# The feed-forward of the first two chunks as one wide pass behind step 4, with weight products spread over steps 0 to 3

## The chip, the core and the metric

The kernel runs on one core of a Trainium2 chip. A core has TensorE (PE in the profile, matrix products; PEld are its weight loads), VectorE (DVE), ScalarE (ACT), GpSimd (POOL) and SyncE (SP, which here issues all the DMAs). Each engine works through its own list of instructions in order, and waits at an instruction until what it needs is there. The metric is the time of one execution on the device, in microseconds; the time given is the median of the runs.

## What is computed

Two layers: attention with a local window and a few global keys, and a feed-forward on its output.

```python
scores = q @ k^T / 8 - slope[h] * dist          # B, H, S, D = 4, 8, 768, 64
keep = (j < n_global) | ((i - j >= 0) & (i - j < n_local))   # 8 and 96
a = softmax(where(keep, scores, -1e9));  x = (a @ v) as [3072, 512]
h = (x @ w1) * (x @ w2)                         # w1, w2: 512 x 1024
out = (h @ w3) @ w_out                          # w3: 1024 x 1024, w_out: 1024 x 512
```

There is no nonlinearity between `w3` and `w_out`, so the kernel forms the product of these two once and multiplies `h` by it. The four weights arrive as float64, 8 bytes a number; q, k and v are float32.

## The kernel before, in words

**Two kinds of work.** The 3072 rows are cut into 12 chunks of 256 rows. A chunk has four pairs of heads, and a *step* is two such pairs of one chunk, so there are 24 steps, two to a chunk. Every third chunk begins a sequence (chunks 0, 3, 6, 9) and has smaller windows. Step s consists of:

- `visit(s)` on PE: the values of step s - 1 (L459, L461; their result `v` is split into `xh` on ACT and `xl` on DVE, L63 and L64), then the scores of step s (L406).
- `rows`: on DVE the bias and the row maxima (L421), on ACT the exponentials (L422).
- `softmax`, called by `scale(s)` in the first steps: DVE forms the reciprocal sums (L427, L428), ACT scales the rows (L434), and the keys and values of step s + 1 are asked for (`loads`).
- `turn(s, 0)` and `turn(s, 1)`: PE transposes the rows of one pair each (L447, L449), ACT copies them to SBUF as `ph` (L451). The PSUM tiles of `turn` (`t`, and `v`, which the values use too) have one buffer each.

The feed-forward of a chunk, or of two chunks together, is a generator, `FeedForward.run`. It yields after each *slice* of work, and `slices(k)` takes k slices, which is how PE's gaps inside a step are filled. With 512 columns (two chunks) a slice is 6 products, with 256 columns it is 12. For each of eight blocks f it forms `m` with w1 (ACT copies it to `a`, L168) and `m` with w2 (DVE multiplies the two, L171, and the result is split into `gh` and `gl`), then it multiplies by the folded weight (L178 to L180). One pass has 48 slices at 512 columns, 24 at 256. Numbers are split into a high and a low part, and each product is three (L161 to L163). The pool of accumulators `m` has two buffers, and the weight products below use the same pool.

**The first steps.** Before any feed-forward the weights have to be made. `convert` loads pieces of 128x512 as float64 and turns them into float32 with three DVE instructions each (L54, L56, L58). `w3(f)` does this for the two pieces of block f of w3, and `w12(f)`, *unit* f, for block f of w1 and of w2; for the latter ACT rounds the high part (`w1h`, `w2h`, L122) and `lows()` has DVE form the low part (L130). `fold(f, ks)` adds the products k of w3 and w_out for block f on PE (L142, eight folds a block); behind the eighth ACT copies the high part (`wh`, L144) and `low(f)` has DVE form the low part (L147). So `low(f)` is the last reader of the accumulator of block f.

**What sets the order.** `first_steps` is a list written by hand. PE follows it throughout; DVE and SP follow it in the first steps; ACT's order there is the scheduler's, and from the step after them on ACT's is by hand too and DVE's and SP's are the scheduler's. SP issues each load at its place in the list, when the buffer that it fills is free: the float64 pieces go into four `stage` slots or two `raws` slots.

Before the change chunks 0 and 1 have a pass of 256 columns each. Chunk 0's begins in step 3, of which `slices` takes ten, and steps 4 to 7 take ten, ten, nine and nine; from step 8 on passes have 512 columns and a step takes twelve (5, 4, 3).

Of the kernel before, what the change touches and what calls it, by code (L numbers as in the profile page):

```python
# [21 lines left out]
NP = H // 2  # L22
NQ = 2
T = NQ * P
# [3 lines left out]
NFC = DF // P  # L28
# [7 lines left out]
STEP = 2  # L36
# [9 lines left out]
def convert(nc, pieces):  # L46


    for dst, raw, src in pieces:
        nc.sync.dma_start(out=dst if src.dtype == F32 else raw, in_=src.bitcast(I32))  # L50
    pieces = [(dst, raw.rearrange("p (n t) -> p n t", t=2)) for dst, raw, src in pieces if src.dtype != F32]

    for dst, w in pieces:
        nc.vector.tensor_scalar(out=dst, in0=w[:, :, 1], scalar1=3, scalar2=0x3FFFFFF8, op0=ALU.logical_shift_left, op1=ALU.bitwise_and)  # L54
    for dst, w in pieces:
        nc.vector.scalar_tensor_tensor(out=dst, in0=w[:, :, 1], scalar=-0x40000000, in1=dst, op0=ALU.bitwise_and, op1=ALU.bitwise_or)  # L56
    for dst, w in pieces:
        nc.vector.scalar_tensor_tensor(out=dst, in0=w[:, :, 0], scalar=29, in1=dst, op0=ALU.logical_shift_right, op1=ALU.bitwise_or)  # L58


def split(nc, hi, lo, x):

    nc.scalar.activation(hi, x, AF.Copy)  # L63
    nc.vector.tensor_tensor(out=lo, in0=x, in1=hi.bitcast(F32), op=ALU.subtract)  # L64


class FeedForward:
# [25 lines left out]
    def next(self, ring, slots):  # L93
        self.turn[ring] += 1
        return slots[(self.turn[ring] - 1) % len(slots)]

    def weights(self, *names):


        pieces, fresh = [], []  # L100
        for kind, *at in names:
            if kind == "w":
                f, n = divmod(at[0], 2)

                raw = self.stage[{3: 0, 5: 2, 6: 0}[f] + n] if f in (3, 5, 6) else self.raws[:, n]
                dst, src = self.t3s[:, at[0] % 4], self.src[n][f]
                fresh.append((n, f, dst.bitcast(F32).rearrange("p (i m) -> p i m", i=NCC)))
            elif kind == "o":
                dst, src = self.wo[:, at[0]], self.w_out[at[0]]
            else:  # L110
                f, z = at
                dst = self.mp.tile([P, PC], I32, tag=self.next(0, "agagoo"), name=f"t3_{f}_{z}")
                src = self.w3t[f, :, z * PC:(z + 1) * PC]
                self.t3[f, z] = dst
            if kind != "w":
                raw = self.next(1, self.stage + self.first)
            pieces.append((dst, raw, src))
        convert(self.nc, pieces)
        self.lows()
        for n, f, x in fresh:  # L120
            hi, lo = (w[:, f] for w in self.w[n])
            self.nc.scalar.activation(hi, x, AF.Copy)  # L122
            self.late.append((lo, x, hi))
        if names[0] == ("o", NFC - 2):

            self.first = []
# [198 lines left out]
def banded(ctx, tc, ff, ns, nt, nf, oki, ident, qk, vx):  # L325
# [139 lines left out]
    n = NC * NP // STEP  # L465
    pairs = lambda s: [divmod(STEP * s + i, NP) for i in range(STEP)]
    work = []
    qrs, vrs, phs, xs = {}, {}, {}, {}

    def slices(k):  # L470
        while k > 0 and work:
            if next(work[0], "end") == "end":
                work.pop(0)
            else:
                k -= 1

    def loads(s, keys=True, vals=True):
        if s < n and keys:
            qrs[s] = [load(*p) for p in pairs(s)]
        if s < n and vals:  # L480
            vrs[s] = [load_values(*p) for p in pairs(s)]

    def visit(s):
        if s:
            c, h0 = pairs(s - 1)[0]
            if h0 == 0 and c % 2 == 0:
                xs[c // 2] = [xp.tile([P, NCC, W], F32R, tag=tag, name=f"{tag}_{c}") for tag in ("xh", "xl")]
            uu = ps_v.tile([P, STEP, T], F32, tag="v", name=f"v_{c}_{h0}")
            for i, p in enumerate(pairs(s - 1)):
                values(uu[:, i], *p, vrs[s - 1][i], phs[s - 1][NQ * i:NQ * (i + 1)])  # L490
        ps = [scores(*p, t) for p, t in zip(pairs(s), qrs[s])] if s < n else []
        if s:
            x2 = xs[c // 2]
            xc = [x[:, :, c % 2 * T:][:, :, :T] for x in x2]
            split(nc, *(x[:, h0:h0 + STEP] for x in xc), uu)
            if h0 + STEP == NP and c < 2:
                work.append(ff.run(c, *xc, c * T, T))
            elif h0 + STEP == NP and c % 2:
                work.append(ff.run(c, *x2, (c - 1) * T, W))
        return ps  # L500

    def all_rows(s, ps):
        return [rows(*p, x) for p, x in zip(pairs(s), ps)]

    def turn(s, i, prs):

        phs.setdefault(s, []).extend(flip(*pairs(s)[i], j, prs[i][0]) for j in range(NQ))

    def first_steps():


        ff.more_stages(xp)
        nc.sync.dma_start(out=nt, in_=ns.bitcast(I32).partition_broadcast(P))
        for x in sc[0] + sc[1]:
            nc.vector.memset(x, 0.0)
        biases()
        ff.weights(("t", 0, 0))
        ff.weights(("o", 0))
        ff.fold(0, 0)
        ff.weights(("t", 1, 0), ("t", 2, 0))  # L520
        ff.fold(1, 0)
        ff.fold(2, 0, pool=(ps_v, "v"))
        ff.weights(("o", 1), ("o", 2))
        for k in (1, 2):
            for f in range(3):
                ff.fold(f, k)
        ff.weights(("o", 3), ("t", 0, 1))
        for f in range(3):
            ff.fold(f, 3)
        ff.weights(("t", 1, 1), ("t", 2, 1))  # L530
        loads(0, vals=False)
        ff.weights(("o", 4), ("o", 5))
        ps = visit(0)
        for k in (4, 5):
            for f in range(3):
                ff.fold(f, k)
        ff.weights(("o", 6), ("o", 7))
        loads(0, keys=False)
        prs = all_rows(0, ps)
        for f in range(3):  # L540
            ff.fold(f, 6, 7)

        def w3(f):
            ff.weights(("t", f, 0), ("t", f, 1))

        def w12(f):
            ff.weights(("w", 2 * f), ("w", 2 * f + 1))

        def scale(s):
            for p, r in zip(pairs(s), prs):  # L550
                softmax(*p, *r, nc.scalar)
            loads(s + 1)

        def fold_and_turn(f, s):
            ff.fold(f, 0, 1, 2, 3)
            turn(s, 0, prs)
            ff.fold(f, 4, 5, 6)
            turn(s, 1, prs)
            ff.fold(f, 7)

        w3(3)
        scale(0)
        ff.low(0)
        w3(4)
        ff.low(1)
        ff.low(2)
        w3(5)
        w12(0)
        fold_and_turn(3, 0)
        ff.lows()  # L570
        w3(6)
        prs = all_rows(1, visit(1))
        ff.low(3)
        ff.fold(4, *range(NFC))
        w12(1)
        scale(1)
        ff.lows()
        w3(7)
        ff.low(4)
        fold_and_turn(5, 1)  # L580
        w12(2)
        ff.lows()
        ff.low(5)
        prs = all_rows(2, visit(2))
        ff.fold(6, *range(NFC))
        w12(3)
        scale(2)
        ff.lows()
        ff.low(6)
        fold_and_turn(7, 2)  # L590
        w12(4)
        ff.lows()
        w12(5)
        ff.lows()
        ff.low(7)
        prs = all_rows(3, visit(3))
        w12(6)
        slices(2)
        scale(3)
        ff.lows()  # L600
        w12(7)
        slices(SLICES[3][0] - 2)
        ff.lows()
        for i in range(STEP):
            turn(3, i, prs)
            slices(SLICES[3][i + 1])
        fits(nc, ff.mp, nf, oki)


    SLICES = [()] * 3 + [(4, 4, 2)] * 3 + [(4, 3, 2)] * 2 + [(5, 4, 3)] * (n - 8)  # L610
    with tc.manual_schedule(engines={mybir.EngineType.PE}):
        with tc.manual_schedule(engines={mybir.EngineType.DVE, mybir.EngineType.SP}):
            first_steps()
        with tc.manual_schedule(engines={mybir.EngineType.Activation}):
            for s in range(4, n + 1):
                rs = all_rows(s, visit(s))
                if s == n:
                    break

                slices(2)  # L620
                for p, r in zip(pairs(s), rs):
                    softmax(*p, *r, nc.vector)
                loads(s + 1)
                slices(SLICES[s][0] - 2)
                for i in range(STEP):
                    turn(s, i, rs)
                    slices(SLICES[s][i + 1])
            slices(10 ** 6)


# [43 lines left out]
```

## Time and profile before

| what | value |
|---|---|
| median of three runs | 596.42 us (596.34 to 596.58) |
| the profiled execution: its time | 596.74 us |
| its span, first to last instruction | 595.0 us |
| PE busy | 573.7 us |
| DVE busy | 260.9 us |
| ACT busy | 284.4 us |
| moved by DMA | 54.01 MB |
| PE's idle time by its waits | 14.7 us, 11.2 of them at the start |

A row of a timeline is: start in us from the span's beginning, length in us, engine, line, operation, output and inputs, shape, count of merged instructions, and in brackets how long the engine idled before and what released it. The start of the next row tells how long an instruction really held its engine, since the lengths of neighbours overlap. A product of full float32 is two records. A row of the busy times by stretch has, behind the stretch, its length and the busy us of PE, PEld, DVE, ACT and POOL (with counts), the granted clock of PE as a share of full speed, the share of the DMA engines and GB/s. A row of the waits says who waited at which line for whom: us in total, times, the longest. Lines are those of the kernel before; up to L490 the changed kernel has the same numbers.

### The profile page before, as it was taken

The numbers are of one execution on the slowest core, as the hardware profiler recorded it, in microseconds if no ns is written. First come the engines' busy times: TensorE is split into PE (matmuls) and PEld (weight loads), VectorE is DVE, ScalarE is ACT, GpSimd is POOL, SyncE is SP. The second block draws the span as 40 slices with busy tenths as digits, with TensorE's granted clock in tenths as the row PEclk, the third lists the DMA queues.
The fourth block names the chain that finished last, engine by engine and source line by source line (L and its number), as shares of the span: only waits on it lengthen the run. The fifth ranks groups of instructions, "written<-read, shape, count | busy, mean of one in ns | idle before, by whom it ended". The sixth has DMA issues, their size and how long they took to land. (4 is left out here: it accounts for less than half of the span.)

```text
span 595.0 us, 9954 instructions
## 1 busy us (share of the span) xinstructions
PE 573.7 (96%) x3872; PEld 459.2 (77%) x3872; DVE 260.9 (44%) x851; ACT 284.4 (48%) x777; POOL 1.3 (0%) x10
## 2 busy tenths in 40 slices
PE   2999998999999999999999999999999999999995
PEld 0444568989988888888888888888888888888884
DVE  8999998531434424404533322541343353112200
ACT  3056677644656446526635544653553663422210
POOL 0000000000000000000000000000000000000000
PEclk9999998999999999999999999999999999999999
DMA  8897752221133202212210330120331020000011
GB/s 305 302 356 238 275 194 106 81 82 33 49 97 98 79 2 78 81 49 69 79 59 21 115 113 3 63 63 14 120 97 49 30 80 19 36 18 1 0 37 40
DMA packets 23240, 54.01 MB, mean 91 GB/s; under 512 B 2704, under 2 KB 4752, under 8 KB 23184
## 3 DMA queue, kind: packets, MB, share of 16 engines
q1 hardware_dynamic: 23184, 53.29, 26.2%
q8 instruction: 32, 0.52, 0.4%
q14 instruction: 24, 0.20, 0.1%
HBM read 46.99 MB, written 6.29 MB: 90 GB/s over the span
## 5 line engine op out<-in xcount | busy, mean ns | idle before, releaser
L422 ACT ACTIVATE pr<-pr,mx 128x232 f32<-128x232 f32 (+1 forms) x192 | 88.4, 462 | 48.7 <-DVE mx L421 48.7
L171 DVE TENSOR_TENSOR g<-m,a 128x512 f32<-128x512 f32 x48 | 33.2, 691 | 133.2 <-PE m L163 132.5
L161 PE MATMUL m<-xh,w1h 128*128 128x512 f32 (+1 forms) x224 | 84.6, 378 | 0.0
L163 PE MATMUL m<-xh,w1l 128*128 128x512 f32 (+1 forms) x224 | 81.0, 361 | 0.0
L162 PE MATMUL m<-xl,w1h 128*128 128x512 f32 (+1 forms) x224 | 80.9, 361 | 0.0
L161 PE MATMUL m<-xh,w2h 128*128 128x512 f32 (+1 forms) x224 | 80.8, 361 | 0.0
L162 PE MATMUL m<-xl,w2h 128*128 128x512 f32 (+1 forms) x224 | 80.4, 359 | 0.0
L163 PE MATMUL m<-xh,w2l 128*128 128x512 f32 (+1 forms) x224 | 80.4, 359 | 0.0
L178 PE MATMUL o<-wh,gh 128*128 128x512 f32 x192 | 76.6, 399 | 0.0
L63 ACT ACTIVATE gh<-g 128x512 fp32r<-128x512 f32 x48 | 30.3, 630 | 94.2 <-DVE g L171 93.6
L180 PE MATMUL o<-wh,gl 128*128 128x512 f32 x192 | 74.9, 390 | 0.0
L179 PE MATMUL o<-wl,gh 128*128 128x512 f32 x192 | 74.9, 390 | 0.0
L142 PE MATMUL w<-wo,t 128*128 128x512 f32 x128 | 59.6, 615 | 11.7 <-DVE wo L58 11.2
L64 DVE TENSOR_TENSOR xl<-v,xh 128x512 fp32r<-128x512 f32 x24 | 16.6, 690 | 120.4 <-ACT xh L63 120.3
L451 ACT ACTIVATE ph<-t 128x512 f32<-128x512 f32 (+1 forms) x96 | 50.1, 558 | 30.1 <-PE t L449 18.9
L142 PEld LDWEIGHTS w<-wo,t 128*128 128x128 f32 x128 | 24.0, 196 | 40.4 <-issue 24.2
L421 DVE CUSTOM_DVE_ANT_0 pr<-s,biasw 128x232 f32<-128x232 f32 x160 | 53.4, 394 | 0.0
L161 PEld LDWEIGHTS m<-xh,w1h 128*128 128x128 f32 x224 | 42.7, 191 | 8.5 <-issue 3.3
L64 DVE TENSOR_TENSOR gl<-g,gh 128x512 fp32r<-128x512 f32 x48 | 33.2, 692 | 33.2 <-ACT gh L63 33.2
L161 PEld LDWEIGHTS m<-xh,w2h 128*128 128x128 f32 x224 | 42.3, 189 | 7.0 <-issue 0.7
L163 PEld LDWEIGHTS m<-xh,w1l 128*128 128x128 f32 x224 | 42.6, 190 | 6.5
L162 PEld LDWEIGHTS m<-xl,w2h 128*128 128x128 f32 x224 | 42.3, 189 | 6.4
(84 smaller groups left out, 815.7 us busy)
## 6 DMA issues: line engine op xcount, KB each, us to landing
qr<-qk SPq DMA_DIRECT2D x32, 312.0 KB, 4.1
vr<-vx SPq DMA_DIRECT2D x32, 256.0 KB, 2.9
stage<-w3t SPq DMA_DIRECT2D x15, 512.0 KB, 6.4
out_dram<-ot SPq DMA_DIRECT2D x24, 256.0 KB, 2.0
raws<-w SPq DMA_DIRECT2D x10, 512.0 KB, 5.6
qr<-qk SPq DMA_DIRECT2D x16, 260.0 KB, 3.3
vr<-vx SPq DMA_DIRECT2D x16, 192.0 KB, 2.6
stage<-w SPq DMA_DIRECT2D x6, 512.0 KB, 6.2
```

The costliest lines, as they stand in the source:

```text
L64: nc.vector.tensor_tensor(out=lo, in0=x, in1=hi.bitcast(F32), op=ALU.subtract)
L142: nc.tensor.matmul(ps, lhsT=self.t3[f, z][:, i * P:(i + 1) * P].bitcast(F32), rhs=self.wo[:, k].bitcast(F32), start=k == 0, stop=k == NFC - 1)
L161: nc.tensor.matmul(ps[:, z], lhsT=mh, rhs=xh[:, i], start=i == 0, stop=False)
L162: nc.tensor.matmul(ps[:, z], lhsT=mh, rhs=xl[:, i], start=False, stop=False)
L163: nc.tensor.matmul(ps[:, z], lhsT=ml, rhs=xh[:, i], start=False, stop=i == NCC - 1)
L171: nc.vector.tensor_tensor(out=g, in0=ps, in1=a, op=ALU.mult)
L178: nc.tensor.matmul(ps, lhsT=gh[:, f, ts], rhs=self.wh[:, f], start=f == 0, stop=False)
L179: nc.tensor.matmul(ps, lhsT=gh[:, f, ts], rhs=self.wl[:, f], start=False, stop=False)
L180: nc.tensor.matmul(ps, lhsT=gl[:, f, ts], rhs=self.wh[:, f], start=False, stop=f == NFC - 1)
L421: nc.vector.tensor_tensor_reduce(out=pr[:, j, u, w0:], in0=ps[u][:, j, w0:UW], in1=bias, scale=-SCALE, scalar=3.0e38, op0=ALU.add, op1=ALU ...
L422: nc.scalar.activation(pr[:, j, u, w0:], pr[:, j, u, w0:], AF.Exp, bias=m, scale=-1.0, accum_out=sm[:, j, u:u + 1])
L451: nc.scalar.activation(ph[:, :, :nk], pt[:, :, :nk], AF.Copy)
```

## The change

Chunks 0 and 1 no longer have passes of their own: one pass of 512 columns serves both, like all the others, and it begins after `visit(4)`. Every step from 4 on takes 5, 4 and 3 slices, and step 3 takes none. `fold_and_turn` gives way to `around`, which puts given folds ahead of, between and behind the two turns of a step; the folds of blocks 3 to 7 are spread over steps 0 to 3. In the list, units of w1 and w2 and blocks of w3 stand at other places, and units 2, 4 and 5 use the `stage` slots where 3, 5 and 6 did.

```diff
-                raw = self.stage[{3: 0, 5: 2, 6: 0}[f] + n] if f in (3, 5, 6) else self.raws[:, n]
+                raw = self.stage[{2: 0, 4: 2, 5: 0}[f] + n] if f in (2, 4, 5) else self.raws[:, n]
...
-            if h0 + STEP == NP and c < 2:
-                work.append(ff.run(c, *xc, c * T, T))
-            elif h0 + STEP == NP and c % 2:
+            if h0 + STEP == NP and c % 2:
                 work.append(ff.run(c, *x2, (c - 1) * T, W))
...
+        def around(s, a, b, e):
+            for i, part in enumerate((a, b, e)):
+                for f, k0, k1 in part:
+                    ff.fold(f, *range(k0, k1 + 1))
+                if i < STEP:
+                    turn(s, i, prs)
         w3(3)
         scale(0)
         ff.low(0)
+        ff.low(2)
         w3(4)
         ff.low(1)
-        ff.low(2)
+        around(0, [(3, 0, 1)], [(3, 2, 2)], [(3, 3, 4)])
         w3(5)
+        prs = all_rows(1, visit(1))
+        ff.fold(3, 5, 6, 7)
+        ff.low(3)
+        scale(1)
         w12(0)
-        fold_and_turn(3, 0)
+        around(1, [(4, 0, 4)], [(4, 5, 5)], [(4, 6, 7)])
         ff.lows()
         w3(6)
-        prs = all_rows(1, visit(1))
-        ff.low(3)
-        ff.fold(4, *range(NFC))
+        prs = all_rows(2, visit(2))
+        ff.low(4)
+        scale(2)
         w12(1)
-        scale(1)
+        around(2, [(5, 0, 7), (6, 0, 0)], [(6, 1, 1)], [(6, 2, 3)])
         ff.lows()
         w3(7)
-        ff.low(4)
-        fold_and_turn(5, 1)
         w12(2)
+        prs = all_rows(3, visit(3))
         ff.lows()
         ff.low(5)
-        prs = all_rows(2, visit(2))
-        ff.fold(6, *range(NFC))
+        scale(3)
         w12(3)
-        scale(2)
+        around(3, [(6, 4, 7), (7, 0, 3)], [(7, 4, 5)], [(7, 6, 7)])
         ff.lows()
         ff.low(6)
-        fold_and_turn(7, 2)
         w12(4)
         ff.lows()
+        ff.low(7)
+        prs = all_rows(4, visit(4))
...
-    SLICES = [()] * 3 + [(4, 4, 2)] * 3 + [(4, 3, 2)] * 2 + [(5, 4, 3)] * (n - 8)
+    SLICES = (5, 4, 3)
...
-            for s in range(4, n + 1):
+            for s in range(5, n + 1):
```

Behind `visit(4)` the new list has units 5, 6 and 7 among step 4's slices and turns.

Three places show what that does to the engines' lists. The first is DVE around `low(5)`, the difference of block 5 (its accumulator is `w_518` in the kernel before). Before, from `low(4)` to the split behind visit 2:

```order
L147 TENSOR_TENSOR wl<-w_465,wh 128x512
L54 TENSOR_SCALAR t3s<-raws 128x512 x2
L56 SCALAR_TENSOR_TENSOR t3s<-raws,t3s 128x512 x2
L58 SCALAR_TENSOR_TENSOR t3s<-raws,t3s 128x512 x2
L130 TENSOR_TENSOR w1l<-t3s,w1h 128x512
L130 TENSOR_TENSOR w2l<-t3s,w2h 128x512
L147 TENSOR_TENSOR wl<-w_518,wh 128x512
L64 TENSOR_TENSOR xl_410<-v_2_565,xh_409 128x2x256
```

And in the change, where the accumulator of block 5 is `w_603`:

```order
L421 ISA pr_3_714,mx_3_715<-s_107,biasw 128x232
L421 ISA mx_3_715 128x1
L130 TENSOR_TENSOR w1l<-t3s,w1h 128x512
L130 TENSOR_TENSOR w2l<-t3s,w2h 128x512
L147 TENSOR_TENSOR wl<-w_603,wh 128x512
L427 TENSOR_SCALAR sm_2_705<-sm_2_705 128x4
```

It stood ahead of the rows of step 2 and now stands behind those of step 3 (the first two lines are the last of these rows).

The second place is PE behind a visit's last scores. Before, behind visit 2, with block 6 as `w_618` and block 7 as `w_661`:

```order
L406 MATMUL s_107<-qr_1_499 64x168
L142 MATMUL w_618<-wo,t_6_0_399 128x512 x4
L142 MATMUL w_618<-wo,t_6_1_400 128x512 x4
L142 MATMUL w_661<-wo,t_7_0_507 128x512 x4
L447 MATMUL t_0_0_666<-ident,pr_0_596 128x128
```

In the change, behind visit 3, with block 6 as `w_613` and block 7 as `w_763`:

```order
L406 MATMUL s_107<-qr_3_587 64x168
L142 MATMUL w_613<-wo,t_6_1_510 128x512 x4
L142 MATMUL w_763<-wo,t_7_0_648 128x512 x4
L447 MATMUL t_2_0_768<-ident,pr_2_703 128x128
L449 MATMUL t_2_0_768<-ident,pr_2_703 128x128
```

Block 7's folds moved from step 2 to step 3. In both programs the first fold of block 7 waits for `low(5)` on DVE, whose accumulator it takes over.

The third place is PE in the first pass of the feed-forward, where `m` with w1 is followed by `m` with w2 (the first number in a name, the chunk or the pass, is left out). Before, block 0 of chunk 0:

```order
L161 MATMUL m_0_0_793<-xh_409,w1h 128x256
L162 MATMUL m_0_0_793<-xl_410,w1h 128x256
L163 MATMUL m_0_0_793<-xh_409,w1l 128x256
L161 MATMUL m_0_1_852<-xh_409,w2h 128x256
L162 MATMUL m_0_1_852<-xl_410,w2h 128x256
```

In the change, block 1 of the pass for both chunks:

```order
L161 MATMUL m_1_0_950<-xh_383,w1h 128x512
L162 MATMUL m_1_0_950<-xl_384,w1h 128x512
L163 MATMUL m_1_0_950<-xh_383,w1l 128x512
L161 MATMUL m_1_1_981<-xh_383,w2h 128x512
L162 MATMUL m_1_1_981<-xl_384,w2h 128x512
```

The products are twice as wide and half as many. In the program of the change the first product of `m_1_1` waits for ACT's copy of `m_1_0`, whose accumulator it takes over.

More of the change, by code (lines that the diff above doesn't have):

```diff
@@ L552, in scale @@
             loads(s + 1)
[L554 to L559, printed above, removed]
+        def around(s, a, b, e):
[4 more added lines that the diff above has]
+                    turn(s, i, prs)
         w3(3)
@@ L563, in first_steps @@
         ff.low(0)
+        ff.low(2)
         w3(4)
         ff.low(1)
-        ff.low(2)
+        around(0, [(3, 0, 1)], [(3, 2, 2)], [(3, 3, 4)])
         w3(5)
+        prs = all_rows(1, visit(1))
+        ff.fold(3, 5, 6, 7)
+        ff.low(3)
+        scale(1)
         w12(0)
-        fold_and_turn(3, 0)
+        around(1, [(4, 0, 4)], [(4, 5, 5)], [(4, 6, 7)])
         ff.lows()
         w3(6)
-        prs = all_rows(1, visit(1))
-        ff.low(3)
-        ff.fold(4, *range(NFC))
+        prs = all_rows(2, visit(2))
+        ff.low(4)
+        scale(2)
         w12(1)
-        scale(1)
+        around(2, [(5, 0, 7), (6, 0, 0)], [(6, 1, 1)], [(6, 2, 3)])
         ff.lows()
         w3(7)
-        ff.low(4)
-        fold_and_turn(5, 1)
         w12(2)
+        prs = all_rows(3, visit(3))
         ff.lows()
         ff.low(5)
-        prs = all_rows(2, visit(2))
-        ff.fold(6, *range(NFC))
+        scale(3)
         w12(3)
-        scale(2)
+        around(3, [(6, 4, 7), (7, 0, 3)], [(7, 4, 5)], [(7, 6, 7)])
         ff.lows()
         ff.low(6)
-        fold_and_turn(7, 2)
         w12(4)
         ff.lows()
+        ff.low(7)
+        prs = all_rows(4, visit(4))
         w12(5)
+        slices(2)
+        scale(4)
         ff.lows()
-        ff.low(7)
-        prs = all_rows(3, visit(3))
         w12(6)
-        slices(2)
-        scale(3)
+        slices(SLICES[0] - 2)
         ff.lows()
+        turn(4, 0, prs)
+        slices(SLICES[1])
         w12(7)
-        slices(SLICES[3][0] - 2)
+        turn(4, 1, prs)
+        slices(SLICES[2])
         ff.lows()
-        for i in range(STEP):
-            turn(3, i, prs)
-            slices(SLICES[3][i + 1])
         fits(nc, ff.mp, nf, oki)
-    SLICES = [()] * 3 + [(4, 4, 2)] * 3 + [(4, 3, 2)] * 2 + [(5, 4, 3)] * (n - 8)
+    SLICES = (5, 4, 3)
     with tc.manual_schedule(engines={mybir.EngineType.PE}):
@@ L623, in banded @@
                 loads(s + 1)
-                slices(SLICES[s][0] - 2)
+                slices(SLICES[0] - 2)
                 for i in range(STEP):
                     turn(s, i, rs)
-                    slices(SLICES[s][i + 1])
+                    slices(SLICES[i + 1])
             slices(10 ** 6)
```

## The prediction

> **What bounds the kernel now.** First the page: who is busy, and when in the span.
>
> ```profile
> span 595.0 us, 9954 instructions
> PE 573.7 (96%) x3872; PEld 459.2 (77%) x3872; DVE 260.9 (44%) x851; ACT 284.4 (48%) x777; POOL 1.3 (0%) x10
> PE   2999998999999999999999999999999999999995
> DVE  8999998531434424404533322541343353112200
> ```
>
> TensorE is full from the second slice to the last but one, so what counts is PE time that is not work. But DVE at 44% is a mean over two regimes. The table of busy time by stretch shows them, and where PE's clock fell:
>
> ```profile
> 75.00:90.00 15.00, 15.00 (x125) 10.63 (x124) 14.71 (x39) 11.54 (x28) 0.00 (x0) 1.00 0.52 188
> 105.00:120.00 15.00, 15.00 (x161) 14.39 (x160) 7.40 (x37) 8.64 (x27) 0.00 (x0) 1.00 0.25 80
> ...
> 96.00:98.00 2.00, 2.00 (x11) 2.00 (x10) 2.00 (x4) 2.00 (x6) 0.00 (x0) 0.51 0.00 0
> ```
>
> Up to 90 us both engines are full (DVE 14.71 of 15); after 105 us DVE has half its time free. PE's waits, all of them but two:
>
> ```profile
> PE w L142 <- DVE wo L58: 11.2, 1, 11.2
> PE t L447 <- ACT pr L434: 2.4, 2, 2.1
> ```
>
> The 11.2 us stand at the start, which the change leaves alone. The 2.1 us stand at step 3's first transpose. So in the first 90 us DVE's conversions and attention rows are a second chain, just hidden behind PE's folds and the feed-forward of chunk 0. This is the cover that the change takes apart.
>
> **The change, from the end backwards.** The scores of each visit mark the steps on PE:
>
> ```profile
> 108.64 1.37 PE L406 MATMUL s<-qr 64*64 64x168 f32 x32
> 181.05 1.37 PE L406 MATMUL s<-qr 64*64 64x168 f32 x32
> 352.09 1.37 PE L406 MATMUL s<-qr 64*64 64x168 f32 x32
> 436.53 1.37 PE L406 MATMUL s<-qr 64*64 64x168 f32 x32
> 86.93 0.28 PE L161 MATMUL m<-xh,w1h 128*128 128x256 f32 x1
> ...
> 89.32 0.28 PE L163 MATMUL m<-xh,w1l 128*128 128x256 f32 x1
> ```
>
> They are those of steps 4, 8, 16 and 20. Steps 4 to 7 take 181.05 - 108.64 = 72.41 us now, with 38 slices of feed-forward. In the change they hold 48, with the same chunks and the same turns as steps 16 to 19 have now: 436.53 - 352.09 = 84.44 us. That adds 12.03 us, and step 3 loses its ten slices, 120 products of 256 columns at (89.32 - 86.93) / 20 = 0.120, 14.3 us. The wide form so saves about 2.3 us. From step 8 on nothing changes. Without new waits the change breaks even when step 4's scores start at 108.64 - 12.03 = **96.6 us**; every microsecond by which they are later is lost. The old 2.1 us wait lies before 108.64 and is in this figure.
>
> [...]
>
> **When do step 4's scores start?** Unit costs on DVE, ACT and PE:
>
> ```profile
> 55.01 0.77 DVE L54 TENSOR_SCALAR t3s<-raws 128x512 int32<-128x512 int32 x2
> 58.08 0.18 DVE L427 TENSOR_SCALAR sm<-sm 128x4 f32<-128x4 f32 x1
> 58.66 0.66 DVE L130 TENSOR_TENSOR w1l<-t3s,w1h 128x512 fp32r<-128x512 f32 x1
> 69.58 0.39 DVE L421 CUSTOM_DVE_ANT_0 pr<-s,biasw 128x232 f32<-128x232 f32 x1
> 72.13 0.76 DVE L54 TENSOR_SCALAR t3s<-stage 128x512 int32<-128x512 int32 x2
> ```
>
> ```profile
> 36.74 0.58 ACT L144 ACTIVATE wh<-w 128x512 fp32r<-128x512 f32 x1
> 73.39 0.47 ACT L422 ACTIVATE pr<-pr,mx 128x232 f32<-128x232 f32 x1
> 76.26 3.13 ACT L434 ACTIVATE pr<-pr,sm 128x232 f32<-128x232 f32 x8
> 79.29 1.06 ACT L451 ACTIVATE ph<-t 128x512 f32<-128x512 f32 x2
> 80.25 0.63 ACT L122 ACTIVATE w1h<-t3s 128x512 fp32r<-128x512 f32 x1
> ```
>
> ```profile
> 48.34 10.57 PE L142 MATMUL w<-wo,t 128*128 128x512 f32 x24
> 77.93 0.27 PE L447 MATMUL t<-ident,pr 128*128 128x128 f32 x1
> 78.80 2.74 PE L142 MATMUL w<-wo,t 128*128 128x512 f32 x6
> 83.21 0.45 PE L459 MATMUL v<-ph,vr 128*64 128x128 f32 x4
> 85.17 1.37 PE L406 MATMUL s<-qr 64*64 64x168 f32 x32
> 86.47 0.39 PE L161 MATMUL m<-xh,w1h 128*128 128x256 f32 x1
> ```
>
> DVE: a converted pair of pieces 3.07 (55.01 to 58.08), a step's sums 0.56, a difference (L147, L130, L64) 0.60, a step's rows 2.55, or 2.1 in a first chunk. ACT: the exponentials end 4.2 after the rows begin (73.39 + 0.47 against 69.58), the scalings of a step take 3.0, a copy of L451 or L144 0.5, of L122 0.55. PE: a fold is two records of 0.44, 0.88; a turn 0.87; values 1.96; scores 1.30.
>
> DVE first. Both kernels are alike to 35.3 us. From there to the end of low(5) the new order has seven converted pairs (products 4 to 7, units 0 to 2 of w1 and w2) 21.5, three steps of rows 7.2, fifteen differences (six low, three lows of two, xl at three visits) 9.0 and the sums of steps 1 and 2 1.1: 38.8 us of work. It also waits where it did not, because work that stood between is gone:
> - low(2) now follows low(0), but ACT's copy of w_2 starts at 36.74 and ends at 37.3: 1.4.
> - low(3) follows step 1's rows at once, and its copy stands behind eight exponentials on ACT: 2.3.
> - lows of unit 0: the raw pieces' DMAs are now behind step 2's keys and values on SP's queue, which wait for visit 1 (issued near 47 and not at 35, landing near 52.5 by the 5.6 us of their row below), and the copies of L122 stand behind four copies of turns, which wait for PE: 2.5.
> - sums of step 2, for its exponentials: 0.9.
> - lows of unit 1, in the same place: 2.3.
>
> ```profile
> raws<-w SPq DMA_DIRECT2D x10, 512.0 KB, 5.6
> 35.33 0.66 DVE L147 TENSOR_TENSOR wl<-w,wh 128x512 fp32r<-128x512 f32 x1
> ```
>
> These are 9.4 us. So low(5), counted from low(0) in the second row, ends near 35.3 + 38.8 + 9.4 = 83.5, with some handovers of 0.1 **84.0 us**. No row shows these waits; if ACT and the DMAs were always ready they are 0 and low(5) ends near 74, PE waits for nothing; with each half longer it ends near 88.7. I take the walk's sum, as each is set by an order of instructions that is fixed.
>
> Now PE. Its own work brings it through visit 3 (values from 72.9, after the last copy of step 2's turn) and the rest of product 6 to about 79.7. Product 7 uses the accumulator of product 5, which low(5) reads: PE stands until 84.1, **4.4 us**. Queued behind this wait are turn 3, visit 4 and all of the feed-forward. Then four folds 3.5, a turn 0.87, two folds 1.75, a turn 0.87, two folds 1.75, values 1.96 and 0.1: 94.9 us.
>
> Then the clock. How did it answer an idle PE so far?
>
> ```profile
> 94.62 0.47 PE L447 MATMUL t<-ident,pr 128*128 128x128 f32 x1 [2.14 <-ACT pr L434]
> 97.67 0.41 PE L161 MATMUL m<-xh,w1h 128*128 128x256 f32 x1
> 98.05 0.28 PE L163 MATMUL m<-xh,w1l 128*128 128x256 f32 x1
> 11.23 2.07 PE L142 MATMUL w<-wo,t 128*128 128x512 f32 x2 [11.23 <-DVE wo L58]
> 13.71 11.07 PE L142 MATMUL w<-wo,t 128*128 128x512 f32 x22 [0.41 <-DVE t L58]
> ```
>
> After 2.14 us idle PE ran at half clock from 94.6 to 97.95 (0.51 in the stretch from 96 to 98): 1.65 us lost. After the 11.23 us at the start 24 records took 13.1 us and not 10.6: 2.5 lost. A wait of 4.4 us will cost at least the first; I take 1.65, and 0 and 2.5 as ends. Scores of step 4: 94.9 + 1.65 = **96.6 us**, just the break-even.
>
> [...]
>
> **Step 4 itself** has two new waits. Turn 4 comes after five slices (6.9 us after the feed-forward's start near 97.9), and the scalings of step 4 on ACT stand behind the exponentials, a first copy L168 and two L122 copies that wait for unit 5's conversion: last scaling near 106.1, so about 0.55 us. Then m_1_1 waits for the copy a of m_1_0, since it got the accumulator that m_1_0 just held (g of m_0, which would free the other, is behind unit 6's conversion on DVE); that copy stands behind two scalings' rest and two L451 copies: 1.4 us. Together 1.95; ends 0 (if the scalings come early) and 3.5. Units 5 to 7 are wanted from about 130 us on and are ready by 121: nothing, hidden behind the products of units 0 to 4.
>
> **Sum.** 595.0 + (96.6 - 96.6) + 1.95 = 597.0 us of span. The profiled execution took 596.74 outside its span of 595.0, but the runs' median is 596.42: add 1.42. **598.4 us**, 0.33% slower.
>
> **Rivals.**
> - *The waits shrink* (faster): if ACT and the DMAs answer in 6 us for the 9.4, low(5) ends at 80.6, PE idles 1 us, and its clock holds: 94.9 - 3.4 = 91.5, span 595 - 5.1 + 1.95 = 591.9, 593.3 us. For it: DVE was full to 90 us, so its order was served well. Against: each wait above has an instruction ahead of it on ACT. It decides from a saving of 3 us on.
> - *The clock holds or step 4 does not wait* (same): without the 1.65, or without the 1.95, 596.4 to 596.8. For it: one wait alone shows the fall, and where it stood may have mattered. Against: 2.14 us were enough.
> - *DMAs late too* (much slower): the pieces of units 1, 3 and 6 stand behind 1.1 MB of keys and values; 1.5 us more at unit 1 and the long loss of the clock, 0.85: 600.8 us.
> [...]
>
> **Chances.** Forecast 0.50, waits shrink 0.13, same 0.27, late DMAs 0.10. About 0.2% (1.2 us) is what can be told from no change: faster is the first rival, 0.13; the same the second, 0.27; slower the rest, 0.60. The 80% range goes from 595.3 (1.5 us of the waits less, and no loss of the clock) to 600.7.
>
> **What would show it.** Right: in PE's waits a fold (L142) that waits about 4 us for DVE's L147 near 80 us; a granted clock near 0.5 for some 3 us behind it; step 4's scores at 96 to 97 us and step 8's some 86.4 later; in DVE's waits L147 for ACT's L144 and L130 for L122, together some 8 us. Wrong: low(5) before 81 us, no wait of PE above 2 us, or step 4's scores before 95.

## The result and the profile after

The changed kernel takes 600.42 us (median of 4 runs, 598.36 to 600.81), the kernel before, run beside it on the same chip, 596.5 us (596.34 to 596.7): a ratio of 1.0061, 95% interval 1.0047 to 1.0076. It is slower. The forecast was 598.4 us; the profiled execution took 598.36, the other three 2 us more, and the experiments have to say why.

The page of the changed kernel, to be read beside the page of before:

```profile
span 596.5 us, 9571 instructions
PE 572.5 (96%) x3680; PEld 447.3 (75%) x3680; DVE 260.6 (44%) x847; ACT 287.2 (48%) x781; POOL 1.3 (0%) x10
PE   2999979999999999999999999999999999999995
DVE  8997898764224425304434323542343452112200
```

PE is busy 1.2 us less (572.5 against 573.7) in a span 1.5 us longer: a hole has come into the sixth slice. The waits of PE from 35 us on:

```profile
PE w L142 <- DVE wl L147: 4.3, 1, 4.3
PE m L161 <- ACT a L168: 1.4, 2, 1.1
PE t L447 <- ACT ph L451: 0.6, 2, 0.3
```

The old wait at step 3's transposes (2.1 us, L447 for L434) is gone. In its place block 7's first fold waits for low(5). The timeline of PE has that fold and the scores of steps 3, 4, 5 and 8:

```profile
74.20 1.37 PE L406 MATMUL s<-qr 64*64 64x168 f32 x32
83.48 5.40 PE L142 MATMUL w<-wo,t 128*128 128x512 f32 x8 [4.28 <-DVE wl L147]
95.96 1.37 PE L406 MATMUL s<-qr 64*64 64x168 f32 x32
108.21 0.50 PE L161 MATMUL m<-xh,w2h 128*128 128x512 f32 x1 [1.11 <-ACT a L168]
119.50 1.37 PE L406 MATMUL s<-qr 64*64 64x168 f32 x32
182.87 1.37 PE L406 MATMUL s<-qr 64*64 64x168 f32 x32
```

Step 4's scores start at 95.96, 0.65 us ahead of the break-even of 96.61. Steps 4 to 7 take 182.87 - 95.96 = 86.91 us, where 84.44 was the figure without waits: 2.47 more. From step 8 on the span is 0.32 shorter (413.63 against 413.95). Sum: -0.65 + 2.47 - 0.32 = +1.5 us, the whole difference of the spans. (Since the three parts make up the span, they add up whatever the break-even is. The 0.32 lies behind step 20: steps 8 to 19 take 255.47 us here and 255.48 before.)

The granted clock stands in the busy times by stretch (behind the stretch its length, then PE, PEld, DVE, ACT, POOL, the clock, the DMA share, GB/s):

```profile
82.00:84.00 2.00, 0.52 (x1) 0.30 (x2) 1.93 (x8) 2.00 (x8) 0.00 (x0) 0.99 1.00 389
84.00:86.00 2.00, 2.00 (x4) 0.92 (x3) 1.55 (x4) 2.00 (x6) 0.00 (x0) 0.50 1.02 416
86.00:88.00 2.00, 2.00 (x4) 0.76 (x4) 1.90 (x4) 1.94 (x5) 0.00 (x0) 0.65 1.01 414
```

PE works at half clock right behind the wait, for some 3.4 us. And DVE's waits between 35 and 90 us, the chain that makes low(5) late (all but 0.45 of the 3.8 us stand ahead of low(5)):

```profile
DVE t3s L54 <- DMA raws<-w: 3.8, 5, 1.1
DVE wl L147 <- ACT wh L144: 3.6, 2, 2.2
DVE sm L427 <- ACT pr L422: 0.9, 1, 0.9
DVE w2l L130 <- ACT w2h L122: 0.3, 1, 0.3
```

### The profile page after: what moved, and what is told of

Same layout as the page of the kernel before. It is cut to its first block, busy times and chain, and to the rows that moved or that the text cites. A ratio compares the mean times of both kernels' runs of the same rounds, so it can differ in the third digit from the quotient of the medians.

```text
span 596.5 us, 9571 instructions
## 1 busy us (share of the span) xinstructions
PE 572.5 (96%) x3680; PEld 447.3 (75%) x3680; DVE 260.6 (44%) x847; ACT 287.2 (48%) x781; POOL 1.3 (0%) x10
## 4 chain that ended last, share of the span: by engine, by line
PE 82%; DVE 11%; ACT 4%; DMA 2%; issue 1%; DVEq 0%; ACTq 0%
PE m L161 14%; PE m L162 14%; PE m L163 14%; PE o L178 7%; PE o L180 7%; PE o L179 7%; PE s L406 4%; PE v L459 4%; PE t L447 3%; PE t L449 3%; PE v L461 3%; DVE t L56 2%; DVE t L58 2%; PE w L142 1%; DVE pr L421 1%; ACT pr L422 1%
## 5 line engine op out<-in xcount | busy, mean ns | idle before, releaser
L161 PE MATMUL m<-xh,w1h 128*128 128x512 f32 x192 | 78.9, 411 | 0.3 <-ACT a L168 0.3
L142 PE MATMUL w<-wo,t 128*128 128x512 f32 x128 | 62.1, 630 | 15.9 <-DVE wo L58 11.1
L161 PE MATMUL m<-xh,w2h 128*128 128x512 f32 x192 | 74.8, 390 | 1.1 <-ACT a L168 1.1
L163 PE MATMUL m<-xh,w1l 128*128 128x512 f32 x192 | 75.2, 392 | 0.0
L162 PE MATMUL m<-xl,w1h 128*128 128x512 f32 x192 | 75.1, 391 | 0.0
L162 PE MATMUL m<-xl,w2h 128*128 128x512 f32 x192 | 74.8, 390 | 0.0
L163 PE MATMUL m<-xh,w2l 128*128 128x512 f32 x192 | 74.7, 389 | 0.0
L64 DVE TENSOR_TENSOR xl<-v,xh 128x512 fp32r<-128x512 f32 x24 | 16.6, 692 | 113.8 <-ACT xh L63 113.8
L142 PEld LDWEIGHTS w<-wo,t 128*128 128x128 f32 x128 | 24.3, 200 | 44.8 <-issue 23.3
L421 DVE CUSTOM_DVE_ANT_0 pr<-s,biasw 128x232 f32<-128x232 f32 x160 | 53.6, 396 | 0.0
L184 ACT ACTIVATE ot<-o 128x512 f32<-128x512 f32 x24 | 14.3, 595 | 71.7 <-PE o L180 61.2
L64 DVE TENSOR_TENSOR gl<-g,gh 128x512 fp32r<-128x512 f32 x48 | 33.2, 693 | 33.7 <-ACT gh L63 33.7
L434 ACT ACTIVATE pr<-pr,sm 128x232 f32<-128x232 f32 (+1 forms) x116 | 44.7, 462 | 1.1 <-DVE sm L427 1.1
L161 PEld LDWEIGHTS m<-xh,w1h 128*128 128x128 f32 x192 | 36.1, 188 | 10.6 <-issue 3.7
L161 PEld LDWEIGHTS m<-xh,w2h 128*128 128x128 f32 x192 | 36.0, 188 | 9.1 <-ACT a L168 1.5
```

The source lines that it names most:

```text
L142: nc.tensor.matmul(ps, lhsT=self.t3[f, z][:, i * P:(i + 1) * P].bitcast(F32), rhs=self.wo[:, k].bitcast(F32), start=k == 0, stop=k == NFC - 1)
L161: nc.tensor.matmul(ps[:, z], lhsT=mh, rhs=xh[:, i], start=i == 0, stop=False)
L162: nc.tensor.matmul(ps[:, z], lhsT=mh, rhs=xl[:, i], start=False, stop=False)
L163: nc.tensor.matmul(ps[:, z], lhsT=ml, rhs=xh[:, i], start=False, stop=i == NCC - 1)
L421: nc.vector.tensor_tensor_reduce(out=pr[:, j, u, w0:], in0=ps[u][:, j, w0:UW], in1=bias, scale=-SCALE, scalar=3.0e38, op0=ALU.add, op1=ALU ...
L434: nc.scalar.activation(x, x, AF.Copy, scale=r)
```

## The experiments

In e4, e8_best, e8b, e9 and e12, which issue some transfers apart from their conversion, the lines of the views are higher by up to 10 (L152 for L142), in e2 by 1.

All were timed against the kernel before, in alternation on the same chip. Ratios are to it.

| run | median us | before | ratio, 95% | PE's main waits from 35 us on in the profile, us |
|---|---|---|---|---|
| the change | 600.42 | 596.50 | 1.0061 (1.0047 to 1.0076) | low(5) 4.3, copy a 1.4 |
| e1_again | 599.93 | 596.14 | 1.0067 (1.0055 to 1.0079) | low(5) 4.4, copy a 1.4 |
| e2_refold | 597.74 | 596.14 | 1.0032 (1.0021 to 1.0044) | low(5) 0.8, copy a 1.4 |
| e3_low5 | 600.63 | 596.14 | 1.0070 (1.0052 to 1.0088) | turn 3 2.4, g 2.0 |
| e4_unit2 | 598.30 | 596.14 | 1.0034 (1.0022 to 1.0047) | copy ph 2.1, xl 2.0, g 1.4 |
| e6_pool | 597.69 | 596.58 | 1.0017 (1.0004 to 1.0030) | low(5) 3.6, copy a 1.1 |
| e8b_order | 600.80 | 596.58 | 1.0073 (1.0050 to 1.0096) | copies a 3.6, turn 3 2.1, xl 1.2 |
| e8_best | 598.50 | 596.58 | 1.0045 (1.0032 to 1.0058) | copies a 2.6, turns 1.7, xl 1.5 |
| e9_raws | 599.82 | 596.58 | 1.0070 (1.0043 to 1.0096) | low(5) 2.7, turns 1.6, g 1.4 |
| e10_later | 594.58 | 596.38 | 0.9960 (0.9944 to 0.9976) | copies a 1.3 |
| e11_short | 595.69 | 596.38 | 0.9984 (0.9972 to 0.9995) | low(5) 1.0, g 1.7 |
| e12_short | 594.92 | 596.38 | 0.9978 (0.9964 to 0.9991) | copies a 2.4, turns 1.6 |

**e1_again: the same kernel, for its scatter.** No edit.

> The changed kernel once more, unaltered, to see what sets its two levels (its profiled execution took 598.36 us, the three others 600.4 to 600.8, with mean clocks of 0.994 against 0.991). Theory (clock): the DVE walk and the wait of PE at block 7's first fold (4.3 us) are the same in every execution, and only the stretch at half clock behind it differs: about 3.4 us in the short level, about 7.5 us in the long one. Most times at 600.4, some at 598.4; a profile of the long level shows step 4's scores near 98.0 and the wait still at 4.3. Rival (transfers): in the long level the pieces of unit 1 land later and low(5) ends some 2 us later; a profile of the long level shows a wait of PE above 6 us and the cold stretch unchanged.

Six runs took 598.88 to 600.56; so there are no two clean levels but a scatter of 2 us, and all six lie above the one that was profiled first. The profile of this one (599.12 us):

```profile
83.67 5.94 PE L142 MATMUL w<-wo,t 128*128 128x512 f32 x8 [4.42 <-DVE wl L147]
...
96.69 1.37 PE L406 MATMUL s<-qr 64*64 64x168 f32 x32
```

```profile
80.00:82.00 2.00, 0.00 (x0) 0.00 (x0) 2.00 (x13) 2.00 (x10) 0.00 (x0) 0.85 1.01 361
82.00:84.00 2.00, 0.33 (x1) 0.33 (x2) 1.93 (x7) 2.00 (x10) 0.00 (x0) 0.50 1.02 399
84.00:86.00 2.00, 2.00 (x3) 0.85 (x3) 1.67 (x5) 2.00 (x7) 0.00 (x0) 0.50 1.02 416
86.00:88.00 2.00, 2.00 (x3) 0.68 (x2) 1.90 (x4) 2.00 (x6) 0.00 (x0) 0.50 1.00 406
88.00:90.00 2.00, 2.00 (x10) 1.14 (x9) 2.00 (x5) 0.31 (x1) 0.00 (x0) 0.94 0.14 55
```

The wait is the same 4.4 us, but the clock falls while PE still waits, near 81.4, and stays down to 88.2: 6.8 us and not 3.4. What the loss costs PE is read from the end of the wait to step 4's scores, the same work in four kernels and five profiles: 10.78 us in e2_refold, where the clock holds, 12.48 in the change's profile, 13.02 here (96.69 - 83.67), 13.66 in e6_pool and 13.81 in e9_raws. So the price is **1.7 to 3.0 us**, and it differs between the two profiles of the same kernel too (1.70 and 2.24). That is for the clock theory, but with a smaller difference (0.5 us) than it had named, and no execution above 600 us was traced. Nor is the clock all of the scatter: the run of 598.88 has a mean clock of 0.996 and is longer than that of 598.36 with 0.994.

**e2_refold: more work in the wait.** The first four products of block 6 are done once more (the first time closed as a sum of its own, `stop` at product 3).

```diff
-        around(3, [(6, 4, 7), (7, 0, 3)], [(7, 4, 5)], [(7, 6, 7)])
+        around(3, [(6, 0, 7), (7, 0, 3)], [(7, 4, 5)], [(7, 6, 7)])
```

> The first four products of block 6 are done twice, the second time where PE now stands and waits for low(5): 3.5 us more work on PE, nothing else changed. Theory (clock): the idle time falls from 4.3 to about 0.8 us, low(5) still ends near 83.4, the clock holds, so the 1.7 us of the short level and the 3.8 us of the long one are both saved: span 594.8, time 596.6, and all runs on one level. Rival 1 (the clock does not hang on this wait): span 596.5 and times of 598.4 to 600.8 as in the change. Rival 2 (the waits come from PE's own order): the added work is paid in full, 602 us and more.

597.74 us, 2.2 less than the change in the same session, with 3.5 us more work on PE. All six mean clocks are 0.997 to 0.999, against 0.991 to 0.996 of the change. In the profile (L143 is L142 here):

```profile
83.46 3.70 PE L143 MATMUL w<-wo,t 128*128 128x512 f32 x8 [0.77 <-DVE wl L148]
94.24 1.37 PE L407 MATMUL s<-qr 64*64 64x168 f32 x32
```

The fold starts at 83.46 as before, since low(5) sets it, and step 4 is 1.7 us earlier, all of it clock. That the wait itself is DVE's and the loss behind it is the clock's is thereby shown; the time is 1.1 us above the 596.6 expected.

**e3_low5: the late instruction moved up.**

```diff
         ff.lows()
+        ff.low(5)
         w3(7)
         w12(2)
         prs = all_rows(3, visit(3))
         ff.lows()
-        ff.low(5)
         scale(3)
```

> low(5) is moved ahead of product 7's conversion, so it ends near 72.8 and not 83.4. Theory (the stall moves on): PE's wait of 4.3 us for low(5) is gone, but turn 3 then waits for its scalings, which stand behind rows of step 3 that have become 0.6 us later: a wait of 2.2 to 3.2 us at L447 for L434 near 82.7, and the clock falls behind it as it did after 2.1 us in the kernel before. Step 4's scores near 94.5, span 595.0, time 596.9 at the short level and 599 at the long one. Rival (low(5) is the whole cause): no new wait, clock holds, scores of step 4 near 90.0, span 590.5, time 592.4.

600.63 us, no gain. PE's timeline:

```profile
85.85 0.34 PE L447 MATMUL t<-ident,pr 128*128 128x128 f32 x1 [2.37 <-ACT pr L434]
95.16 1.37 PE L406 MATMUL s<-qr 64*64 64x168 f32 x32
108.61 0.50 PE L161 MATMUL m<-xh,w2h 128*128 128x512 f32 x1 [1.99 <-DVE g L171]
```

The stall went where it was expected, to turn 3, with 2.37 us, and took the clock along (0.51 from 86 to 88 us). A second one was not expected: with low(5) elsewhere the pool gives m_1_1 the accumulator that g of m_0 frees, and g stands behind unit 6's conversion; 1.99 us idle there were enough for a second stretch at half clock (0.50 from 110 to 112).

**e4_unit2: one conversion later.** `w12(2)` goes behind `scale(3)`; its transfers are issued at the old place.

> Unit 2 of w1 and w2 is converted behind step 3's rows, low(5) and sums, and not ahead of them; its transfers are issued where they were. Theory (DVE's total is the bound, not the place of one instruction): low(5) ends near 79.2 and PE waits for nothing in step 3, so step 4's scores start near 90.0; but DVE's work up to low(7) is the same sum, so step 4's xl and rows come near 95 and 98: the feed-forward's first product with xl waits about 2.7 us for L64, and turn 4 about 2 us for its scalings. Span 594.7 to 598 (as the clock holds or falls), so 4.5 of the 6 us are given back. Rival (only low(5) was late): no new wait above 1 us in step 4, span 590.5, time 592.4.

598.3 us, span 597.4. The fold no longer waits, and three others do:

```profile
90.57 0.45 PE L469 MATMUL v<-ph,vr 128*64 128x128 f32 x4 [2.09 <-ACT ph L461]
97.72 0.50 PE L172 MATMUL m<-xl,w1h 128*128 128x512 f32 x1 [2.01 <-DVE xl L65]
108.78 0.50 PE L171 MATMUL m<-xh,w2h 128*128 128x512 f32 x1 [1.41 <-DVE g L181]
```

The wait for xl was expected (2.7). The one for ph was not: on ACT a copy of turn 3 stood behind unit 3's copy (L132), which waited for unit 3's conversion on DVE. e3 and e4 together: whatever DVE did later, something else that hangs on DVE was late next. But the order is not without effect: e4 is 1.6 us faster than e1_again in the same session, and the intervals of the two ratios do not overlap.

**e9_raws: transfers or copies?** `fetch(0)` and `fetch(1)`, the transfers alone, are issued ahead of `scale(1)` and `scale(2)`.

> The transfers of units 0 and 1 of w1 and w2 are issued ahead of the keys and values of steps 2 and 3, and not behind them; all else is the change. It tells apart what DVE waits for there: it waited 1.06 and 0.85 us for unit 0's pieces and 0.56 and 0.84 for unit 1's, and then not at all for unit 0's copies of L122. Theory (two lateness in a row): the waits for transfers go, but the copies of L122 stand behind four copies of turns on ACT and end as before, so that L130 waits instead; low(5) still ends near 83.4 (82.5 at the earliest), time as the change, 599 to 600. Rival (only the transfers were late): the 3.3 us are gained, low(5) near 80.1, PE waits 1 us, clock holds, time 594 to 595.

599.82 us, as the change. The waits for the pieces of units 0 and 1 (3.3 us) are gone, and low(5) starts at 82.22 and not at 82.71. But not L130 took them over, as expected: DVE now reaches the rows of steps 2 and 3 before PE does, and waits there.

```profile
60.30 0.69 DVE L65 TENSOR_TENSOR xl<-v,xh 128x512 fp32r<-128x512 f32 x1 [1.29 <-ACT xh L64]
77.86 0.69 DVE L65 TENSOR_TENSOR xl<-v,xh 128x512 fp32r<-128x512 f32 x1 [1.18 <-ACT xh L64]
```

PE's visit 2 itself was later (scores at 59.56 and not 58.10, 0.4 of it from the start of the execution), because ACT now makes unit 0's copies ahead of turn 1's copies.

**e11_short: less work on DVE.** That DVE's sum is the bound is tested by taking some of it away.

```diff
-    for dst, w in pieces:
+    for dst, w in pieces if full else ():        # full: not for w1, w2
         nc.vector.scalar_tensor_tensor(out=dst, in0=w[:, :, 0], scalar=29, ...)
```

> The change, without the third pass of the conversion (L58) for w1's and w2's units: the lowest three bits of their mantissas are left out, DVE has 1.2 us less work a unit and no other engine has more. Theory (DVE's sum up to low(5) is the bound): unit 0's 1.2 us are lost again to unit 1's transfer, units 1 and 2 leave 2.4: low(5) ends near 81.0, PE waits 1.9 us and not 4.3; 2.4 us gained, and 1.7 to 2.2 more in those runs in which the clock holds: 595.5 to 597.5. Rival (the waits on transfers and ACT are the bound, not the work): low(5) ends at 82.5 or later, 599 to 600.

595.69 us: 4.2 us less than e1_again's median, and 0.7 less than the kernel before. low(5) starts at 80.84, PE waits 0.97 us for it, and the clock is 0.997 to 0.999 in all twelve runs. 1.2 us less a unit on DVE, with no order changed, is worth the whole loss of the change. (It leaves out bits of w1 and w2, so it isn't a better version.)

**e6_pool: the work moved instead.** `self.nc.gpsimd` for `self.nc.vector` in `lows`.

> The differences of w1's and w2's units (L130) are done by GpSimd and not by DVE; DVE's order is otherwise the change's. Theory (DVE's sum up to low(5) is the bound): 3 units' differences, 3.6 us, leave DVE ahead of low(5), of which unit 0's 1.2 are lost again to unit 1's transfer (landed at 66.4 and 67.7); low(5) ends near 80.5, PE waits 1.4 us and not 4.3, the clock holds, step 4's scores near 91.4, span 592, time 594: faster than both kernels. Rival (GpSimd is slow, or slows DVE): no row of GpSimd with such an operation is there; if one takes 3 us or DVE's conversions get longer beside it, the conversion of unit u+2 waits for unit u's differences and nothing is gained, 599 to 600.

597.69 us (595.01 to 599.1): some 2 us better than the change, and not better than the kernel before. In the profile, that of one of the longer executions (599.02), low(5) starts at 82.60 and PE waits 3.55 us. Two views of it show why so little came of it, GpSimd's and DVE's:

```profile
57.00 4.08 POOL L130 TENSOR_TENSOR w1l<-t3s,w1h 128x512 fp32r<-128x512 f32 x1 [55.10 <-ACT w1h L122]
61.04 1.27 POOL L130 TENSOR_TENSOR w2l<-t3s,w2h 128x512 fp32r<-128x512 f32 x1
71.34 1.32 POOL L130 TENSOR_TENSOR w1l<-t3s,w1h 128x512 fp32r<-128x512 f32 x1 [9.04 <-ACT w1h L122]
72.63 1.45 POOL L130 TENSOR_TENSOR w2l<-t3s,w2h 128x512 fp32r<-128x512 f32 x1
```

```profile
71.12 1.83 DVE L54 TENSOR_SCALAR t<-stage 128x512 int32<-128x512 int32 x2
72.87 2.36 DVE L56 SCALAR_TENSOR_TENSOR t<-stage,t 128x512 int32<-128x512 int32 x2
76.36 0.75 DVE L54 TENSOR_SCALAR t3s<-stage 128x512 int32<-128x512 int32 x2
77.04 1.28 DVE L56 SCALAR_TENSOR_TENSOR t3s<-stage,t3s 128x512 int32<-128x512 int32 x2
```

A difference takes GpSimd 1.27 us. Beside two of them DVE's pairs take 1.83 and 2.36 us and not 0.75 and 1.28: each is about 1.1 us longer, and the first difference of all takes 4.08 us, beside DVE's conversion passes. So these two kinds of instruction were longer beside each other, by 1.1 and 2.8 us. DVE's rows (L421, 0.39 us) and its differences of a PSUM tile (L64 at 79.45, 0.67 us) keep their length beside GpSimd's. L54 and L56 read only from SBUF, while L64 and L421 have one input in PSUM; no run here shows whether that makes the difference.

**e8b_order and e8_best: the order rewritten.** low(5) as in e3; unit 3 converted behind turn 3; low(7) ahead of unit 4, `scale(4)` ahead of unit 5, units 5 and 6 fetched early; step 5's exponentials ahead of its split. e8_best has GpSimd's differences as well.

> Order alone, with the same work on each engine: low(5) ahead of product 7's conversion; unit 3 converted behind turn 3; low(7) and the sums of step 4 ahead of units 4 and 5; step 5's exponentials ahead of its copy of x. Theory (DVE's sum is the bound): as in the run with low(5) alone, turn 3 waits about 2.3 us for its scalings and the clock may fall, but the second wait there (2.0 us for L171) and the wait for the copy behind unit 3 are gone: span 594.5 to 596, time 596.5 to 598, no better than the kernel before. Rival (the order is the bound, not the sum): no wait above 1 us, span 591, time 593.

> The reordered kernel with the differences of w1's and w2's units on GpSimd as well. Theory: DVE's sum is then short enough that low(5) ends near 71, step 3's rows end near 80.5 and turn 3 does not wait; step 4's scores near 90.2, waits of at most 2 us in step 4 and none in step 5; the clock holds: span 590.5 to 592.5, time 592.3 to 594.3, some 2 to 4 us faster than the kernel before. Rival (GpSimd slow): as without GpSimd or worse, 597 and more.

600.8 and 598.5 us. Order alone gains nothing (turn 3 2.07, xl 1.22, copies a 3.6, of which 3.0 in step 5). e8_best has step 4's scores at 91.77, 4.2 us ahead of the change, and gives 3.0 of it back by step 8 (181.65 against 182.87) with waits for xl (1.52) and copies a (2.6). Both miss their expectation. e8b_order's wait in turn 3 is what the theory of the sum had foreseen; the 3.0 us for a copy on ACT are not, and whether they come of DVE's sum or of ACT's order stays open. e8_best was too hopeful about GpSimd.

**e12_short: that order with less work.** e8b_order without L58 for w1's and w2's units.

> The reordered kernel (low(5) ahead of product 7's conversion, unit 3 behind turn 3, and so on) without L58 for w1's and w2's units, lowest three bits left out as well. Theory (order pays once DVE's sum is shorter): step 3's scalings come 2 us sooner, turn 3 waits 0.3 us at most, the clock holds, step 4's scores near 91, the waits of the reordered kernel in step 4 and 5 (1.2 for xl, 0.6 and 3.0 for copies a) shrink to 2 us in all: span 592 to 594, time 594 to 596. Rival (the copies on ACT are the bound by now, and its order): the 3.0 us at step 5's copy a stay, 597 and more.

594.92 us, step 4's scores at 90.92, and waits of 4.0 us in all left from 35 us on: copies a 2.4 (1.8 of them in step 5), turns 1.6. Against e11_short the order is good for 0.8 us by the medians at most, and the two intervals overlap, so no gain of the order is shown: part of the rival's point, the copies on ACT, holds.

**e10_later: the same lesson applied to the kernel before.** It too waits once for DVE's and ACT's rows, with a lost clock behind it, and there PE has other work at hand.

```diff
-    SLICES = [()] * 3 + [(4, 4, 2)] * 3 + [(4, 3, 2)] * 2 + [(5, 4, 3)] * (n - 8)
+    SLICES = [()] * 3 + [(6, 2, 2)] + [(4, 4, 2)] * 2 + [(4, 3, 2)] * 2 + [(5, 4, 3)] * (n - 8)
```

> The kernel before, with step 3's first turn after six slices of feed-forward and not four (the second after two more, as before, then two). Theory (a wait and the clock behind it are PE time that work can fill): the scalings that PE waited 2.14 us for are done 0.7 us ahead of the turn's new place, the wait and the stretch at half clock are gone: 2.1 + 1.65 = 3.8 us less, span 591.2 and 592.5 to 593 in time, mean clock 0.998 or more in every run. Rival (it only moves): the copies of turn 3 come 2.9 us later and the values of step 4 or the accumulators wait instead; span 594 or more.

**594.58 us, ratio 0.9960 (0.9944 to 0.9976): faster than both kernels.** PE's timeline has the waits that remain:

```profile
93.02 0.39 PE L161 MATMUL m<-xh,w1h 128*128 128x256 f32 x1 [0.25 <-ACT a L168]
98.05 0.39 PE L161 MATMUL m<-xh,w2h 128*128 128x256 f32 x1 [1.01 <-ACT a L168]
106.83 1.37 PE L406 MATMUL s<-qr 64*64 64x168 f32 x32
```

The 2.14 us and the stretch at half clock are gone, all clocks are 0.997 or more, and 1.3 us came back as waits for copies a behind the scalings on ACT. 1.8 us were gained of the 3.8 expected. One more reason: the runs of the kernel before have mean clocks of 0.994 to 0.999, with spans from 597.2 down to 593.6, so it doesn't lose the clock in every execution, and the 1.65 us were not there to be won each time.

## Why the prediction was right, and where it was not

- **Break-even at 96.6.** Held as far as it can be read: steps 4 to 7 exceed the 84.44 us of the wide form by 2.47 us, and what PE waited there accounts for 2.4 of them (below).
- **The walk of DVE.** low(5) was to end at 84.0; it ended at 83.4. This is nearer than its parts: DVE's waits were 1.3 us fewer than forecast, and the rest of the walk took 40.1 us where 39.3 had been counted. PE's own work was to end at 79.7; it ended at 79.2. The wait was to be 4.4 us; it is 4.28.
- **The 9.4 us of waits in that walk.** Measured 8.1 (1.36, 2.23, 1.91, 0.88, 1.40 and 0.31 in the order of the list). The terms for the lows of units 0 and 1 were too large (4.8 us, measured 3.6) and half wrong in cause: the prediction gave them to late transfers and to copies of L122 together; 3.3 us were the transfers and 0.3 the copies. e9_raws shows that the other cause didn't stand ready behind it either: the next in line was PE's own visit. The rival by which the waits shrink had said that 3 us less there would decide. In e9_raws 3.3 us of them were gone and low(5) started 0.5 us earlier, which shows what it left out: PE, DVE and ACT wait for each other in turn in steps 1 to 3, so DVE can't run far ahead.
- **The clock.** The term of 1.65 us was right for the first profile of the change (1.70) and too small for the second (2.24) and for two of the experiments (2.9 and 3.0). This is the mis-sized term. The upper bound of 2.5 was too low as well, though the folds behind the wait at the start had been read rightly: two records took 2.07 us together there, at 0.44 each at full speed. (The table by stretch gives a clock of 1.00 for them, but the trace's record of the clock begins only at 16.06 us.) And "2.14 us were enough" is no rule: it depends on where a wait lies, as the last section shows. Together with a scatter in the first 44 us, the clock could account for the missing 2.0 us between 598.4 and the median of 600.42: the first scores (step 1), with the same program ahead of them, start at 43.51 in the change's profile and at 43.56 to 44.25 in the ten experiments that share it. That makes 1.3 and 0.7. The mean clocks of the three longer runs (0.991 and 0.992, against 0.994) fit it, but no single execution at 600.4 was traced, so this sum is argued and not shown.
- **Step 4's two waits, 1.95.** 1.11 us for copy a of m_1_0, as named, and 0.5 us in turn 4, whose transposes came one by one behind the scalings from 104.19 to 105.45. With 0.26 at m in step 5 that is 1.9. The rest is in the same two waits. Set beside steps 16 and 17 of the kernel before, the products behind the wait of 1.11 us start 1.4 us later, and those behind the wait of 0.26 us 0.55 later: idle time is counted from the modelled end of the product ahead, which lies behind the start that the next one would have had. That makes 2.4 of the 2.47.
- **The rivals.** The clock that holds would have given 596.4 to 596.8; e2_refold is that case, and with the 3.5 us of filling for free it took 597.7. The clock fell in both profiles of the change, behind waits of 4.28 and 4.42 us, and in e3_low5 behind 1.99 us. The late transfers' rival names the time nearest to the median (600.8), but low(5) came no later than forecast: DVE waited 1.4 us for unit 1's pieces, within that term's 2.3. Only its longer loss of the clock came true.
- **Where luck helped.** The profiled execution lies within 0.1 us of the forecast because its misses cancel: step 4's scores 0.65 earlier, step 4 0.5 longer, 0.3 less behind step 8, and 1.86 us of time outside the span where 1.42 had been added. The median lies 2.0 us above the forecast, near the upper end of the range.

The mechanism was therefore the forecast one: the feed-forward of chunk 0 had been the cover of DVE's conversions, and without it PE reaches step 4 with 14.3 us less work behind it while DVE's work is the same. e11_short shows it from the other side.

## What to carry to other kernels

Before work is taken out of the stage of the busiest engine, add up what the second engine must finish in that stage. If the sum doesn't fit, another order of the same work moves the wait: here two orders gained nothing against the change (e3, e8b), one took back 1.6 us (e4), and none reached the kernel before; less work on the second engine did (e11). A wait of PE of some 2 us or more can cost up to 3 us again through its clock (1.7 to 3.0 behind the waits of 2.7 to 4.4 us for low(5); e8b_order's 3.00 us cost nothing), so work that fits into the wait was better than free here (e2), and a transpose that came two slices later paid (e10). A kernel whose first steps hang on waits can scatter more between runs than its profile lets one think: the one profiled execution lay at the low end of the scatter and made the forecast look 2 us better than it was.

## What was not expected of the hardware

The granted clock falls at different times behind or within the same wait: 84.0 us in one execution and near 81.4 in another, for 3.4 and 6.8 us, with 4.3 and 4.4 us of idleness. In the records of the clock of the kernel before and of the change, the falls come 23 and 20 times 3.413 us behind the first record (94.57 and 83.97 us, behind 16.06 and 15.70). The two falls of e3_low5, near 86.03 and at 109.94 us, lie 7 times 3.41 apart, and in all eight profiles with a fall of the clock between 40 and 130 us half clock lasted 3.41 or 6.83 us. So the changes lie on a grid of 3.41 us, which begins elsewhere in each execution. What separates the cases in these eight is how long PE was busy in one such stretch, and not how long it waited. Between 40 and 130 us, full clock gave way to half clock behind all nine stretches with 1.44 us busy or less, and behind none with 1.54 or more. e3_low5's wait of 1.99 us lies in one stretch; e8b_order's of 3.00 us, which ended at 129.11, is cut in two and cost no clock (here each row is one stretch):

```profile
106.52:109.94 3.42, 1.44 (x7) 1.11 (x7) 2.72 (x6) 3.04 (x6) 0.00 (x0) 1.00 0.39 133
109.94:113.35 3.41, 3.41 (x10) 2.67 (x9) 1.45 (x4) 0.00 (x0) 0.00 (x0) 0.50 0.45 174
```

```profile
129.11 0.50 PE L171 MATMUL m<-xh,w1h 128*128 128x512 f32 x1 [3.00 <-ACT a L178]
123.86:127.28 3.42, 2.25 (x10) 1.51 (x9) 3.35 (x27) 2.60 (x11) 0.00 (x0) 1.00 0.02 5
127.28:130.69 3.41, 1.58 (x7) 1.27 (x8) 2.47 (x8) 3.41 (x11) 0.00 (x0) 1.00 0.01 2
130.69:134.10 3.41, 3.41 (x21) 2.92 (x20) 0.69 (x1) 2.09 (x4) 0.00 (x0) 1.00 0.00 0
```

The full clock came back behind stretches that PE filled (3.36 to 3.41 us busy), and not behind those with 1.14, 2.42 and 2.70 us busy (e1_again, e6_pool, e9_raws): there half clock lasted 6.83 us. By these figures, which are those of one family of kernels, a wait of 4 us would lose the clock wherever the grid lies (an estimate from them: cut in two, it would still leave 1.41 us busy or less in one stretch of 3.41), and one of 2 or 3 us may.

GpSimd's subtraction of 128x512 numbers takes 1.27 us alone (e6_pool), but pairs of DVE's conversion passes that met it took about 1.1 us longer, and one of GpSimd's that met them took 4.08 us, so that moving 0.6 us of DVE's work to GpSimd can cost DVE more than that.
